# Transposing two chunks of normalised rows by SBUF-to-SBUF transfers, with another list of VectorE's score groups

## The chip, the cores and the metric

The kernel runs on one core of a Trainium2 chip. The metric is the device time of one execution in microseconds, the median of three runs. A core has five engines that run side by side and meet only at semaphores: TensorE (PE, matmul), VectorE (DVE), ScalarE (ACT, exponentials and the like), GpSimd (POOL) and SyncE (SP), which here only issues transfers. Each engine works off its own list of instructions in order.

## The reference

A block with layer norm, attention and a gated multilayer perceptron over 2048 rows of 448 numbers in bf16:

```python
xn = _layernorm(x, axis=-1)
s = _A_ref(xn, A_wqkv, A_wo)      # 16 heads of 28, softmax over 2048 keys
g = _silu(_B_ref(xn, B_w1, B_b1, B_w2, B_b2))   # 448 -> 1792 -> gelu -> 448
return x + s * g
```

Inside `_A_ref`: `qkv = x @ wqkv`, scores `q . k` times 28 to the power -0.5, softmax, times `v`, times `wo`. The largest part is the exponentials: 16 x 2048 x 2048 of them.

## The kernel before, in words

**Tiling.** The 2048 rows are four chunks `c` of 512 rows, each of four tiles `t` of 128 rows. The 16 heads are four groups `g` of four heads; a head takes 32 rows of the 128, so that four heads' scores can run on four row strips of TensorE. A block is one group and one chunk of queries; 16 blocks make the attention. Within a block a score tile `m` is 128 keys times 512 queries of one head, in a bank of PSUM; there are 16 x 16 x 4 = 1024 of them (`MTOT`).

**Start.** `p_ln` computes mean and variance of a chunk's rows on VectorE, `p_ln2` normalises the four tiles into `xn` (VectorE the even tiles, GpSimd the odd ones from chunk 1 on; lines L706 and L710). `xn` lies inside the buffer `h` and has three slots, chunk `c` in slot `c % 3`. The matmuls need the features on the partitions, so `xn` is transposed into `xnT`: for chunk 0 in `p_first`, for chunks 1 to 3 in `p_tr`, twice per chunk: eight TensorE transposes against the identity into one PSUM bank (`t_tr`, L724) and one VectorE copy of 128 x 1024 to `xnT` (`t_trev`, L735). Then `p_k`, `p_q` and `p_v0` project keys, queries and values (L744, L1031), with VectorE evicting them (L755, L983, L1041). Later the rest of the projections and the first layer of the perceptron (`p_f1`, matmul L1089, eviction L1072) are worked in between the scores.

**Exponentials.** `p_scores` (L1223) puts two or three score tiles in one of the two halves of the PSUM ring; `p_exps` lets ScalarE exponentiate such a unit in one instruction (L1279) into a slot of `P`, or later of `h` and `xnT`. `p_pv` multiplies with the values into `acc` (L1494).

**VectorE's groups.** `QUADS` lists the groups of four score tiles (`m = 4q` to `4q + 3`) whose exponential VectorE computes instead of ScalarE: `p_late` sends their scores to any free bank, `p_apass` evicts each with a scale and an offset as 16-bit integers (L1382), and `p_expq` finishes the four together with five operations (L1433 to L1440).

**What sets the order.** The order of every engine's instructions is fixed before the launch by a planner (`run`): each piece of work is a Python generator that yields tasks with a planned duration; the planner puts the task that could start first, with priorities, and emits the waits on semaphores that follow from the buffers (`deps`, `mark`). Tasks that wait for a transfer use a planned time of landing. `until` conditions are tested against planned times. An engine then runs its list in that order whatever the real times are. Transfers are issued by SyncE in the order in which they were planned; a wait holds up all that is behind it in that list.

**Transfers.** At the start SyncE issues all loads of `x`, `wqkv`, then `b2`, `w1` (1344 KB and 224 KB), then copies of `x` into the output for the final addition; `wo` follows once GpSimd has cleared it, `w2` late.

**End.** `p_epi` and `p_norm4` normalise a block, `p_out` and `p_last` multiply by `wo`, multiply by the gate and add to the output.

Of the kernel before, what the change touches and what calls it, by code (L numbers as in the profile page):

```python
# [11 lines left out]
PE, ACT, DVE, POOL, SP = ET.PE, ET.Activation, ET.DVE, ET.Pool, ET.SP  # L12
# [7 lines left out]
C = 4  # L20
# [7 lines left out]
MTOT = NBLK * T * 4  # L28

GM = 64 * 9 + 6  # L30
QUADS = (17, 22, 25, 36, 37, 59, 65, 72, 82, 87, 99, 103, 115, 122, 129, 135, 138, 142, 152, 153, 157, 158, 164, 168, 178, 180, 194, 199, 211, 213, 222, 229, 234, 242)
SM_SCALE = DH ** -0.5
LOG2E = 1.4426950408889634
EXP_A3, EXP_A2, EXP_LC = 0.16391228, 0.00783292, 1.1187538523466403
# [12 lines left out]
SEM, OWN = 0.07, 0.03  # L47
SWITCH = 0.1
JOINT = 0.05
LEAD, WAIT, GLEAD = 0, 3.0, 48  # L50
EPS = 0.1

# [24 lines left out]
class _Kernel:  # L77
# [183 lines left out]
    def alloc(self):  # L261
# [117 lines left out]
        self.s_x = [self.sem("s_x%d" % q) for q in range(4)]  # L379
        self.s_x2 = [self.sem("s_x2%d" % q) for q in range(4)]  # L380
        self.s_b1 = self.sem("s_b1")
        self.s_qn = [[self.sem("s_qn%d_%d" % (q, c)) for c in range(C)] for q in range(G)]
        self.s_x0b, self.s_wqk1 = self.sem("s_x0b"), self.sem("s_wqk1")
        self.s_out = [self.sem("s_out%d" % q) for q in range(10)]
# [2 lines left out]
    def schedule(self):  # L387
        K = self
        K.n_f1 = 0
        K.exp_u = -1  # L390
        K.exp_m = -1
        K.late_ready = []
        K.sc_u = -1
        K.pv_m = -1
        K.E_done = -1
        K.norms_done = False
        K.stg_done = 0
        K.qsqs = [0, 1]
        K.qn = [[] for _ in range(G)]
        K.qn_done = 0  # L400
        K.q0_done = 0
        K.f2n = [0] * C
        K.pv_started = False
        K.chunks_done = 0
        K.g_done = [False] * C
        K.on_done = [False] * NBLK
        K.on4 = [False] * 4
        K.ln_done = 0
        K.taken = 0
        K.next_m = 0  # L410
        K.n_late = 0
        K.gu = None
        K.pend = None
        K.units = []
        K.pv_done = [False] * MTOT
        K.late = {4 * q + k for q in QUADS for k in range(4)}
        K.late_left = [sum(1 for q in QUADS if K.sub_of(4 * q) == b) for b in range(NBLK + 3)]
        K.late_on = False
        K.PB, K.PPREV, K.plast = {}, {}, {}
        K.free_u = []  # L420
        K.a_left = {}
        K.ln2e = 0
        K.late_blk = 0
        K.banks += [(K.ring[:, b, :], K.b_ring[b]) for b in (3, 2)]
        K.outs = []
        K.gelu_done = False
        K.dir_n = 0
        K.dir_read = 0
        self.constants()
        self.loads()  # L430
        for c in range(C):
            K.spawn(K.p_ln(c), c)
        K.spawn(K.p_first(), 0)
        K.spawn(K.p_scores(), 0)
        K.spawn(K.p_take(2), 0)
        K.spawn(K.p_exps(), 0)
        K.spawn(K.p_pv(), 0)
        K.spawn(K.p_units(), 0)
        K.spawn(K.p_late(), 0)
        K.spawn(K.p_busy(), 100)  # L440
        o = 1.0

        def nxt():
            nonlocal o
            o += 1.0
            return o
        K.spawn(K.p_norms(), nxt())
        for c in range(1, C):
            K.spawn(K.p_tr(c, 0), nxt())
            K.spawn(K.p_tr(c, 1), nxt())  # L450
            K.spawn(K.p_k(0, c), nxt())
            if c == 1:
                K.spawn(K.p_v0(0), nxt())
            K.spawn(K.p_v0(c), nxt())
        K.spawn(K.p_q(0, 1), nxt())
        for c in (2, 3):
            K.spawn(K.p_q(0, c), nxt())
        for c in range(C):
            K.spawn(K.p_k(1, c), nxt())
        K.spawn(K.p_q(1, 0), nxt())  # L460
        for t in range(T):
            K.spawn(K.p_v1(t), nxt())
        for c in (1, 2, 3):
            K.spawn(K.p_q(1, c), nxt())
        K.spawn(K.p_qn(1), nxt())
        f1 = deque(SBT)
        for c in range(C):
            for _ in range(4):
                K.spawn(K.p_f1(*f1.popleft()), nxt())
            K.spawn(K.p_k(2, c), nxt())  # L470
            K.spawn(K.p_q(2, c), nxt())
        K.spawn(K.p_qn(2), nxt())
        while f1:
            K.spawn(K.p_f1(*f1.popleft()), nxt())
        for c in range(C):
            K.spawn(K.p_k(3, c), nxt())
            K.spawn(K.p_q(3, c), nxt())
        K.spawn(K.p_qn(3), nxt())
        K.spawn(K.p_gelu(), 0)
        K.spawn(K.p_direct(), 0)  # L480
        for c in range(C):
            for t in range(4):
                K.spawn(K.p_f2(c, t), nxt())
            K.spawn(K.p_silu(c), nxt())
        K.o_epi = 0.5
        for c in range(C - 1):
            for t in range(4):
                K.spawn(K.p_out(c, t), nxt())
        for t in range(4):
            K.spawn(K.p_last(t), nxt())  # L490
        K.run()
        for h in K.outs:
            K.wait(SP, h)
# [92 lines left out]
    def loads(self):  # L586
        K = self

        def ld(dst, src, sem, w, land):
            return K.dma(SP, lambda eng: eng.dma_start(dst, src), sem, writes=w, land=land)  # L590
# [16 lines left out]
            ld(K.x_sb[:, c, :, :], xr[c], K.s_x[c], [K.b_x[c]], 8.0 + 1.8 * c)  # L607
        lw(4 * DH, D, K.s_wqk1, K.b_stg1, 16.5)

        ld(K.b2b[:, :], K.B_b2.partition_broadcast(128), K.s_w["b"], [K.b_b2], 20)  # L610
        ld(K.w1[:, 0:3, :], K.B_w1[0:384, :].rearrange("(kt p) f -> p kt f", p=128), K.s_w["w1"], [], 0)
        ld(K.w1[0:64, 3, :], K.B_w1[384:448, :], K.s_w["w1"], [K.b_w1], 30)

        def out_x():
            yield ("until", lambda: K.late_on)
# [67 lines left out]
    def p_ln2(self, c, h, ts):  # L683
        K = self
        sl = slice(4 * c + ts[0], 4 * c + ts[-1] + 1)
        if c < 2:
            yield _Task(ACT, lambda eng: eng.activation(K.lnv[:, sl], K.mv[:, sl, 1], ACTF.Ln, bias=K.epsc[:, 0:1]),
                        [K.b_mv[c][h], K.b_pads], [K.b_ln[c][h]], 0.3, 0.0, 2 if c else 0)
            yield _Task(ACT, lambda eng: eng.activation(K.rstd[:, sl], K.lnv[:, sl], ACTF.Exp, scale=-0.5),
                        [K.b_ln[c][h]], [K.b_rs[c][h]], 0.2, 0.0, 2 if c else 0)  # L690
        else:
            yield _Task(POOL, lambda eng: eng.tensor_scalar(K.lnv[:, sl], K.mv[:, sl, 1], LN_EPS, None, op0=ALU.add),
                        [K.b_mv[c][h]], [K.b_ln[c][h]], 0.24, 0.05, 0)
            yield _Task(POOL, lambda eng: eng.tensor_tensor(K.rstd[:, sl], K.lnv[:, sl],
                                                            K.mhalf[:, 0:1].to_broadcast([128, len(ts)]), ALU.pow),
                        [K.b_ln[c][h], K.b_pads], [K.b_rs[c][h]], 1.1, 0.05, 0)
        if len(ts) == 4:
            K.b_rs[c][1] = K.b_rs[c][0]
        if c > 0:
            yield _Task(POOL, lambda eng: eng.tensor_scalar(K.nm[:, sl], K.mv[:, sl, 0], -1.0, None, op0=ALU.mult),  # L700
                        [K.b_mv[c][h]], [K.b_nm[c][h]], 0.22, 0.05, c)
        for t in ts:
            i = 4 * c + t
            rd = [K.b_x0[h] if c == 0 else K.b_x[c], K.b_mv[c][h], K.b_rs[c][h], K.b_pads]
            if c == 0 or t % 2 == 0:
                yield _Task(DVE, lambda eng, i=i, t=t: eng.tensor_scalar(  # L706
                    K.xn[:, c % 3, t, 0:D], K.x_sb[:, c, t, :], K.mv[:, i, 0:1], K.rstd[:, i:i + 1],
                    op0=ALU.subtract, op1=ALU.mult), rd, [K.b_xn[c % 3][t]], 0.38, 0.05, c)
            else:
                yield _Task(POOL, lambda eng, i=i, t=t: eng.tensor_scalar(  # L710
                    K.xn[:, c % 3, t, 0:D], K.x_sb[:, c, t, :], K.nm[:, i:i + 1], K.rstd[:, i:i + 1],
                    op0=ALU.add, op1=ALU.mult), rd + [K.b_nm[c][h]], [K.b_xn[c % 3][t]], 0.7, 0.05, c)
        K.ln_done += len(ts) // 2

    def t_tr(self, c, pr, h, bank, tok, prio=5):
# [240 lines left out]
    def p_tr(self, c, pr):  # L956
# [5 lines left out]
        K.banks.append((bank, tok))  # L962
        K.chunks_done += 1

    def boot(self):
        return self.b_qT[0][1].tw is not None

# [358 lines left out]
    def may_join(self, r):  # L1326
# [7 lines left out]
        st = K.start_of(p["task"])  # L1334
        return st is not None and max(r["tok"].tr, r["tok"].tw or 0.0) + SEM <= st + JOINT

# [15 lines left out]
    def p_late(self):  # L1352
        K = self
        yield ("until", lambda: K.late_on)
        K.spawn(K.p_room(), 0)
        for q in QUADS:
            m0 = 4 * q
# [325 lines left out]
```

## Time and profile before

The time is 461.31 us, the median of three runs (460.98 to 461.32). The profiled execution spans 459.3 us.

| what | before |
|---|---|
| time | 461.31 us |
| TensorE busy | 436.3 us, 95%, of it 34.3 us of filler matmuls (L905) |
| VectorE busy | 373.1 us, 81% |
| ScalarE busy | 446.8 us, 97% |
| GpSimd busy | 40.9 us, 9% |
| exponentials on ScalarE (L1279) | 362 instructions, 418.8 us busy |
| TensorE transposes of chunks 1 to 3 (L724) | 48, median 219 ns |
| their VectorE copies (L735) | 6 of about 0.69 us |
| VectorE's group evictions (L1382) | 136 of about 0.69 us |

Busy time counts an instruction from its start to its end, and neighbouring instructions of an engine overlap a little. A row of the groups by line names the line of the program, the engine, the operation, what it writes and reads, its shape, how often it ran, and its busy time and mean. In the timeline the first two numbers of a row are the start and the length in microseconds; `x6` after the names means that six instructions in sequence are merged in the row. A row of the windows gives, for a stretch of time, its length and each engine's busy time and number of instructions. A row of the waits names who waited, for whom, the total, how often, and the longest.

### The profile page before, as it was taken

How to read it: one execution, taken by the hardware profiler on the slowest of the kernel's cores; microseconds unless marked ns; L12 is line 12 of the kernel's file. 1: busy time of each engine (PE TensorE's matmuls, PEld its weight loads, DVE VectorE, ACT ScalarE, POOL GpSimd, SP SyncE). 2: the span in 40 equal slices, each digit the busy share in tenths (PEclk: the TensorE clock that was granted, in tenths of full speed). 3: DMA queues.
4: the chain of work that ended last, by engine and by line, in shares of the span. 5: the costliest groups of instructions: out<-in, count | busy, mean ns of one | idle time of the engine just before them, and what ended most of it. 6: DMA issues, size and time to landing. Idle time of an engine off the chain costs nothing.

```text
span 459.3 us, 10615 instructions
## 1 busy us (share of the span) xinstructions
PE 436.3 (95%) x4431; PEld 162.2 (35%) x4431; DVE 373.1 (81%) x584; ACT 446.8 (97%) x408; POOL 40.9 (9%) x85
## 2 busy tenths in 40 slices
PE   6999999999999999999999999999999999989994
PEld 5543333333332323323333333333323334343452
DVE  8956898894897798878989989847778978999965
ACT  5999999999999999999999999999999999999994
POOL 7470000000000000000000000000000100101111
PEclk9999999999999999999999999999999999999998
DMA  8701000000000000000050000000000001300331
GB/s 269 268 2 37 2 0 1 1 1 4 1 1 0 1 2 3 1 2 1 0 143 1 2 0 2 1 1 0 1 1 2 1 0 42 43 1 1 42 43 41
DMA packets 8050, 11.16 MB, mean 24 GB/s; under 512 B 1698, under 2 KB 6994, under 8 KB 7955
## 3 DMA queue, kind: packets, MB, share of 16 engines
q1 hardware_dynamic: 6850, 8.43, 6.1%
q0 software_dynamic: 864, 1.38, 2.4%
q8 instruction: 35, 0.57, 0.5%
q10 hardware_dynamic: 288, 0.69, 0.4%
q14 instruction: 13, 0.10, 0.1%
HBM read 8.61 MB, written 3.21 MB: 26 GB/s over the span
## 4 chain that ended last, share of the span: by engine, by line
PE 47%; ACT 38%; issue 11%; DVE 3%; POOL 1%; ACTq 0%; DVEq 0%; POOLq 0%
ACT P L1279 18%; PE ring L1223 13%; ACT xnT L1279 9%; ACT h L1279 9%; PE acc L1494 8%; PE ring L1089 5%; PE ring L1158 3%; PE misc L1158 3%; PE acc L905 3%; PE misc L1089 2%; PE misc L744 2%; PE ring L744 2%; PE acc L887 1%; PE misc L1223 1%; PE ring L1031 1%
## 5 line engine op out<-in xcount | busy, mean ns | idle before, releaser
L1279 ACT ACTIVATE P<-ring 128x1024 bf16<-128x1024 f32 (+1 forms) x188 | 217.6, 1265 | 1.4 <-PE ring L1223 1.0
L1223 PE MATMUL ring<-qT,kT 32*128 32x512 bf16 (+2 forms) x1074 | 145.1, 358 | 11.4 <-ACT P L1279 5.6
L1279 ACT ACTIVATE h<-ring 128x1024 bf16<-128x1024 f32 (+1 forms) x102 | 117.8, 1268 | 0.2
L1223 PEld LDWEIGHTS ring<-qT,kT 32*128 32x128 bf16 x1074 | 37.6, 91 | 134.2 <-ACT P L1279 55.7
L1279 ACT ACTIVATE xnT<-ring 128x1536 bf16<-128x1536 f32 (+1 forms) x72 | 83.4, 1308 | 0.0
L1494 PE MATMUL acc<-P,vaug 128*32 128x512 bf16 (+2 forms) x524 | 49.2, 358 | 0.0
L1089 PE MATMUL ring<-xnT,w 128*128 128x512 bf16 x156 | 41.4, 382 | 1.1 <-ACT h L1138 0.9
L1564 POOL CAST rhi<-rc 128x16 bf16<-128x16 f32 x15 | 6.0, 400 | 365.2 <-DVE rc L1562 297.0
L905 PE MATMUL acc<-ident,zero 128*128 128x128 bf16 x393 | 34.3, 221 | 0.0
L1223 PE MATMUL misc<-qT,kT 32*128 32x512 bf16 (+1 forms) x78 | 29.1, 376 | 0.0
L905 PEld LDWEIGHTS acc<-ident,zero 128*128 128x128 bf16 x393 | 22.3, 97 | 18.8 <-issue 18.2
L1494 PE MATMUL acc<-h,vaug 128*32 128x512 bf16 x248 | 27.6, 384 | 0.0
L1158 PE MATMUL misc<-w,h 128*128 128x448 bf16 x112 | 27.3, 356 | 0.0
L1158 PE MATMUL ring<-w,h 128*128 128x448 bf16 x112 | 27.2, 355 | 0.0
L1382 DVE TENSOR_SCALAR x_sb<-misc 128x512 uint16<-128x512 f32 x31 | 21.3, 686 | 6.2 <-PE misc L1223 5.9
L1089 PE MATMUL misc<-xnT,w 128*128 128x512 bf16 x68 | 19.5, 383 | 0.5 <-DVE qT L1581 0.5
L1552 DVE CAST E_sb<-acc 128x512 bf16<-128x512 f32 x15 | 10.4, 690 | 11.7 <-PE acc L1494 11.7
L1494 PE MATMUL acc<-xnT,vaug 128*32 128x512 bf16 (+2 forms) x240 | 18.7, 330 | 0.9 <-ACT P L1279 0.7
L1089 PEld LDWEIGHTS ring<-xnT,w 128*128 128x128 bf16 x156 | 12.1, 97 | 20.0 <-issue 7.2
L1494 PEld LDWEIGHTS acc<-P,vaug 128*32 128x32 bf16 x524 | 11.8, 94 | 15.0 <-issue 11.8
L1382 DVE TENSOR_SCALAR kT<-ring 128x512 uint16<-128x512 f32 x19 | 13.1, 688 | 4.3 <-PE ring L1223 3.4
L1138 ACT ACTIVATE h<-h 128x2048 bf16<-128x2048 bf16 (+2 forms) x8 | 16.2, 2029 | 0.0
(269 smaller groups left out, 663.2 us busy)
## 6 DMA issues: line engine op xcount, KB each, us to landing
w<-in_B_w_dram SPq DMA_DIRECT2D x1, 1568.0 KB, 7.6
w<-in_B_w_dram SPq DMA_DIRECT2D x1, 1344.0 KB, 8.6
out_dram<-in_A_x_dram SPq DMA_DIRECT2D x3, 448.0 KB, 10.7
out_dram<-h POOLq DMA_DIRECT2D x6, 224.0 KB, 3.9
x_sb<-in_A_x_dram SPq DMA_DIRECT2D x2, 448.0 KB, 5.0
h<-in_A_wqkv_dram SPq DMA_DIRECT2D x3, 168.0 KB, 5.1
x_sb<-in_A_x_dram ACTq DMA_DIRECT2D x1, 448.0 KB, 4.4
h<-in_A_x_dram SPq DMA_DIRECT2D x1, 448.0 KB, 4.3
```

What stands on the lines that cost most here:

```text
L744: ins = eng.matmul(bank, w[:, kt, g * 128:(g + 1) * 128], K.xnT[:, kt, c * 512:(c + 1) * 512], start=(kt == 0), stop=(kt == KT - 1))
L887: yield _Task(PE, lambda eng: eng.matmul(bank[:, 0:256], K.ident[:, :], K.E_sb[:, 0, 0:256], start=True, stop=True), [K.b_id, K.b_pads], [ ...
L905: ins = eng.matmul(K.acc[:, 0:128], K.zero[:, :], K.ident[:, :], start=False, stop=True, skip_group_check=True)
L1089: ins = eng.matmul(bank, K.w1[:, kt, ft * 128:(ft + 1) * 128], K.xnT[:, kt, c * 512:(c + 1) * 512], start=(kt == 0), stop=(kt == KT - 1))
L1138: yield _Task(ACT, lambda eng, dst=dst, src=src: eng.activation(dst, src, ACTF.Gelu_apprx_tanh), rd, wr, 0.4267 * n + (0.1 if pc else 0.06 ...
L1158: ins = eng.matmul(ps, hv[:, ft, t * 128:(t + 1) * 128], K.w2[:, ft, :], start=(ft == 0), stop=(ft == FT - 1))
L1223: return eng.matmul(dst, K.kT[32 * j:32 * j + 32, g, t * 128:(t + 1) * 128], K.qT[32 * j:32 * j + 32, g, c * 512 + q0:c * 512 + q0 + nq], ...
L1279: return eng.activation(reg[:, i0:i0 + n, :], K.ring[:, b0:b0 + n, :], ACTF.Exp, scale=SM_SCALE)
L1382: yield _Task(DVE, lambda eng: eng.tensor_scalar(K.unit[u][:, 512 * k:512 * k + 512].bitcast(dt.uint16), bank, SM_SCALE * LOG2E * 128.0, ( ...
L1494: return eng.matmul(K.acc[32 * j:32 * j + 32, q0:q0 + nq], K.vaug[:, t, 4 * g + j, :], ap[:, col:col + nq], tile_position=(0, 32 * j), sta ...
L1552: yield _Task(DVE, lambda eng: eng.tensor_copy(E, K.acc[:, :]), [K.b_acc], [tE], 0.7, 0.0, 0)
L1564: yield _Task(POOL, lambda eng: eng.tensor_copy(K.rhi[:, :], K.rc[:, :]), [K.b_rc], [K.b_rhl], 1.1, 0.0, 1)
```

## The change

For chunks 2 and 3 the sixteen transposes and two copies of a chunk are replaced by transposing transfers from SBUF to SBUF: one per tile of 128 rows (`p_dtr`), issued by SyncE as soon as the tile is normalised. All four of a chunk count up one semaphore, and the chunk's `xnT` counts as written when the last of them has landed, planned 3.0 us after its tile (`DTL`). This takes the work from TensorE and VectorE. Chunks 0 and 1 stay as they were. So that the transfers don't stand behind the large loads, `b2` and `w1` are loaded after all transposes are issued. The bookkeeping in `xn_c` says which chunk a slot of `xn` holds. The list of VectorE's groups has 33 entries in place of 34; 13 of them are in both lists.

```diff
-QUADS = (17, 22, 25, 36, 37, 59, 65, 72, 82, 87, 99, 103, 115, 122, 129, 135, 138, 142, 152, 153, 157, 158, 164, 168, 178, 180, 194, 199, 211, 213, 222, 229, 234, 242)
+QUADS = (17, 20, 25, 36, 38, 57, 72, 82, 90, 98, 104, 114, 121, 134, 135, 140, 141, 148, 153, 155, 158, 164, 167, 178, 187, 194, 196, 209, 215, 218, 229, 234, 241)
...
+DT, DTL = (2, 3), 3.0
...
         for c in range(1, C):
-            K.spawn(K.p_tr(c, 0), nxt())
-            K.spawn(K.p_tr(c, 1), nxt())
+            if c in DT:
+                K.spawn(K.p_dtr(c), nxt())
+            else:
+                K.spawn(K.p_tr(c, 0), nxt())
+                K.spawn(K.p_tr(c, 1), nxt())
             K.spawn(K.p_k(0, c), nxt())
...
-        ld(K.b2b[:, :], K.B_b2.partition_broadcast(128), K.s_w["b"], [K.b_b2], 20)
-        ld(K.w1[:, 0:3, :], K.B_w1[0:384, :].rearrange("(kt p) f -> p kt f", p=128), K.s_w["w1"], [], 0)
-        ld(K.w1[0:64, 3, :], K.B_w1[384:448, :], K.s_w["w1"], [K.b_w1], 30)
+        def load_w1():
+            yield ("until", lambda: K.chunks_done == 2 * (C - 1))
+            ld(K.b2b[:, :], K.B_b2.partition_broadcast(128), K.s_w["b"], [K.b_b2], K.now + 8)
+            ld(K.w1[:, 0:3, :], K.B_w1[0:384, :].rearrange("(kt p) f -> p kt f", p=128), K.s_w["w1"], [], 0)
+            ld(K.w1[0:64, 3, :], K.B_w1[384:448, :], K.s_w["w1"], [K.b_w1], K.now + 10)
+        K.spawn(load_w1(), 40)
...
+    def p_dtr(self, c):
+        K = self
+        left = [0, 1, 2, 3]
+        while left:
+            yield ("until", lambda: any(K.b_xn[c % 3][t].tw is not None and (c < 3 or K.xn_c[c % 3][t] == c) for t in left))
+            t = min((t for t in left if K.b_xn[c % 3][t].tw is not None and (c < 3 or K.xn_c[c % 3][t] == c)), key=lambda t: K.b_xn[c % 3][t].tw)
+            left.remove(t)
+            last = not left
+            src = K.xn[:, c % 3, t, :].rearrange("n (k p) -> n k p", p=128)
+            dst = K.xnT[:, :, c * 512 + t * 128:c * 512 + (t + 1) * 128]
+            tok = K.b_xn[c % 3]
+            K.deps(SP, [tok[t]], [])
+            K.dma(SP, lambda eng, dst=dst, src=src: eng.dma_start_transpose(dst, src), K.s_tr[c],
+                  reads=tok if last else [], writes=K.b_xnT[c] if last else [], land=max(K.now, tok[t].tw) + DTL)
+            K.chunks_done += 1 if t % 2 else 0
```

More of the change, by code (lines that the diff above doesn't have):

```diff
@@ L381, in alloc @@
         self.s_b1 = self.sem("s_b1")
+        self.s_tr = [self.sem("s_tr%d" % q) for q in range(C)]
         self.s_qn = [[self.sem("s_qn%d_%d" % (q, c)) for c in range(C)] for q in range(G)]
@@ L397, in schedule @@
         K.stg_done = 0
+        K.xn_c = [[-1] * 4 for _ in range(3)]
         K.qsqs = [0, 1]
@@ L703, in p_ln2 @@
             i = 4 * c + t
+            K.xn_c[c % 3][t] = -1
             rd = [K.b_x0[h] if c == 0 else K.b_x[c], K.b_mv[c][h], K.b_rs[c][h], K.b_pads]
@@ L708, in p_ln2 @@
                     op0=ALU.subtract, op1=ALU.mult), rd, [K.b_xn[c % 3][t]], 0.38, 0.05, c)
+                K.xn_c[c % 3][t] = c
             else:
@@ L712, in p_ln2 @@
                     op0=ALU.add, op1=ALU.mult), rd + [K.b_nm[c][h]], [K.b_xn[c % 3][t]], 0.7, 0.05, c)
+                K.xn_c[c % 3][t] = c
         K.ln_done += len(ts) // 2
```

## The prediction

> **What bounds the kernel now.** I read the page's busy shares first, then the windows by stage, then ScalarE's own waits, then the timeline around the place of the change.
>
> ```profile
> PE 436.3 (95%) x4431; PEld 162.2 (35%) x4431; DVE 373.1 (81%) x584; ACT 446.8 (97%) x408; POOL 40.9 (9%) x85
> ```
>
> Two engines are nearly full. TensorE's share holds 34 us of filler matmuls on `acc` (L905, x393), so real matmul work is some 402 us. ScalarE has no filler. By stage:
>
> ```profile
> core 0: us, PE busy (x) PEld busy (x) DVE busy (x) ACT busy (x) POOL busy (x), PEclk, DMA share, GB/s
> 20.00:32.00 12.00, 11.93 (x126) 5.45 (x124) 8.41 (x19) 11.70 (x13) 7.71 (x10) 1.00 0.03 9
> 32.00:45.48 13.48, 13.33 (x109) 4.54 (x111) 7.69 (x15) 13.48 (x15) 3.49 (x4) 1.00 0.15 31
> 276.70:452.80 176.10, 170.44 (x1961) 65.66 (x1959) 140.38 (x198) 175.90 (x156) 11.58 (x20) 1.00 0.08 13
> ```
>
> In these rows ScalarE's column almost equals the width; this holds from the first exponential (12.94 us) to the last (452.18 us), the first 8 us apart. In the stretch that the transposes lie in (20 to 32 us) VectorE is busy only 8.41 of 12 us. ScalarE's own waits behind scores are short:
>
> ```profile
> ACT P L674 <- DMA x_sb<-in_A_x_dram: 2.2, 1, 2.2
> ACT P L1279 <- PE ring L1223: 1.0, 3, 0.5
> ```
>
> The busy column hides small gaps, because one ACTIVATE's tail overlaps the next one's start. The distance between starts is the real price:
>
> ```profile
> 90.49 1.07 ACT L1279 ACTIVATE P<-ring 128x1024 bf16<-128x1024 f32 x1
> 91.39 6.96 ACT L1279 ACTIVATE h<-ring 128x1536 bf16<-128x1536 f32 x6
> 98.24 1.46 ACT L1279 ACTIVATE P<-ring 128x1536 bf16<-128x1536 f32 x1
> 99.57 1.05 ACT L1279 ACTIVATE h<-ring 128x1024 bf16<-128x1024 f32 x1
> ```
>
> A unit of two score tiles takes 0.90 us (90.49 to 91.39), one of three 1.33 us (98.24 to 99.57). The groups by shape give 196 units of two, 165 of three and one of one: 196 x 0.90 + 165 x 1.33 + 0.5 = 396 us for 888 tiles. The time from 12.94 to 452.66 us, less the stretch of GELU and its tables (247.92 to 275.80), the four tanh (6.6) and one layer-norm pair (0.4), is 405 us. So about **8 us of small gaps** are spread over the exponentials. The end is ScalarE's work plus these gaps plus a fixed tail of 6.6 us.
>
> **What the Trainium skill says.** "VectorE: DVE Perf Modes", section "The three transpose paths", lists 390 ns for a 128x128 bf16 transpose on TensorE and 1309 ns for one through the DMA crossbar. The trace has 219 ns for the TensorE one in its pipelined run; no run of before has the other. "DMA: Bandwidth & Descriptors", section "Latency and other measured facts", gives transposing transfers 261 GB/s in one kernel and 350 to 400 when contiguous; nothing in the trace shows it. The same page's "DMA Transpose (X-bar)" demands that only one stream transposes at a time: all eight transfers go out on SyncE, so no wait is added for that. Its section "Why a DMA increments its semaphore by 16 and not by 1" says that of DMAs in flight on one semaphore only the full count proves that all have landed; the change waits for the full count of a chunk's four transfers. The trace can't confirm it.
>
> **The change, part by part.**
>
> *Removed from TensorE and VectorE.*
>
> ```profile
> L724 PE MATMUL misc<-ident,h x24: 218/219/230, 15.2 to 29.5; 128*128 128x128 bf16 x24
> L735 DVE COPY xnT<-misc x3: 673/680/691, 16.7 to 29.8; 128x1024 bf16<-128x1024 bf16 x3
> L735 DVE COPY xnT<-ring x3: 678/692/692, 17.3 to 30.6; 128x1024 bf16<-128x1024 bf16 x3
> ```
>
> Of the 48 transposes, 32 are chunks 2 and 3: eight runs of four at about 0.40 us, 3.2 us of TensorE. Of six copies four go: 4 x 0.69 = 2.7 us of VectorE. Both lie beside ScalarE's exponentials, which run from 21.13 us on without a recorded idle. What is gained on the path is at most the small gaps there: 26 units of two from 21.13 to 45.48 us take 24.35 us against 26 x 0.90 = 23.4 us. Of these 0.9 us I take 0.2 us as gained, since most of the gaps there lie away from the transposes.
>
> *Eight transposing transfers.* Each moves 128 x 512 x 2 B = 131 KB, that is four 128x128 blocks. Low bound: the nearest row, the 112 KB stores of `h`, 1.7 us from issue to landing. High bound: four blocks at the page's 1309 ns one after the other, 5.2 us, with the next transfer behind it. The new code plans 3.0 us after the last tile. Who waits: the K projection of chunk 2, and everything behind it in TensorE's order, scores included.
>
> ```profile
> 20.10 1.03 DVE L706 TENSOR_SCALAR h<-x_sb,mv,rstd 128x448 bf16<-128x448 bf16 x2
> 20.19 1.51 POOL L710 TENSOR_SCALAR h<-x_sb,nm,rstd 128x448 bf16<-128x448 bf16 x2 [0.20 <-POOL nm L700]
> 21.13 14.92 ACT L1279 ACTIVATE P<-ring 128x1024 bf16<-128x1024 f32 x16 [0.30 <-PE ring L1223]
> 23.66 0.68 DVE L735 COPY xnT<-misc 128x1024 bf16<-128x1024 bf16 x1
> 26.09 0.69 DVE L755 CAST kT<-ring 128x512 bf16<-128x512 f32 x1 [0.80 <-PE ring L744]
> 27.87 0.12 PEld L1223 LDWEIGHTS ring<-qT,kT 32*128 32x128 bf16 x2 [0.21 <-issue]
> ```
>
> Chunk 2's last normalised tile is ready at 20.19 + 1.51 = 21.7 us; before, its transpose is complete at 24.34 and its K at 26.78 us. The first score on chunk 2's keys is the 17th unit (four heads times eight key tiles, two to a unit). Counting 1 + 7 units before 21.13 us and 0.92 us for each after it, the 17th exponential starts near 28.5, its score near 27.9 us. The slack is 27.9 - 26.8 = 1.1 us, so the transfers may land until about 24.3 + 1.1 = 25.4 us free of charge. SyncE's issues take about 0.53 us each (two `x_sb` loads in 1.06 us). Four between 20.6 and 22.3 us with 1.7 to 3.2 us to land (the row of a 224 KB load) gives 24.0 to 25.5 us: hidden, just. The high bound gives 20.6 + 4 x 5.2 = 41.4 us: 16 us late. I take 0. Chunk 3 has 1.7 us of slack by the same count (K at 33.57, its first score at 35.3 us).
>
> *The later load of w1, b2 and its place.* It moves from 8.61 us behind the transfers, to near 30 us, and takes 9 us. The first GELU projection is evicted at 102.4 us (L1072), so this costs nothing, nor do the loads of `wo` behind it, which the output projection needs only after 430 us.
>
> *One of VectorE's groups less, the others moved.* The list has 34 entries before and 33 after. A group is four score tiles that VectorE exponentiates (four L1382 of 0.69 us and five operations of 0.69, 0.69, 1.22, 0.69 and 1.22 us, 7.3 us). All four now go to ScalarE. At (0.90 + 1.33) / 5 = 0.446 us per tile that is **+1.78 us** on the engine that sets the end, hidden behind nothing. VectorE had 19% idle before, so the 7.3 + 2.7 us it is freed of buy nothing by themselves. In return the interference of one group goes: the gaps divided by the groups are 8 / 34 = 0.2 us.
>
> *Sum.* +1.8 for the group, -0.2 for its gaps, -0.2 in the start, 0 for the transfers: +1.4 us, 461.3 + 1.4 = **462.7 us**.
>
> **The rivals.**
>
> *A better fit of the groups (faster).* Only 13 of the 33 positions are also in the list before, and the 8 us of gaps depend on where the groups stand. If the gaps fall to 5 us, the result is -3.0 + 1.8 = -1.2 us: 460.1 us. For it: the gaps are bigger than the price of a group, and an early TensorE with 3 us less work lets projections run earlier. Against it: the gaps are scattered and mostly 0.1 to 0.2 us, nothing in the trace ties them to the transposes, and most groups sit in blocks far from them.
>
> *The gaps pay for just the group (no change).* Gaps down by 1.8 us: 461.3 us.
>
> *Late transfers (slower).* The wait on the transpose takes the place of the one on VectorE's copy. If they land 3 us after the slack ends, ScalarE, with at most two units ahead, runs dry and the loss is never made good: 462.7 + 3 = 465.7 us. At the high bound 475 us and more. For it: a slack of only 1.1 us and a price with a ratio of three between its bounds. Against it: transfers share 16 engines, so four in a row need not take four times one.
>
> **How the numbers follow.** Forecast 0.42, better fit 0.28, even 0.12, late transfers 0.18. The forecast's own spread, 461.9 to 463.6 us, gives 0.04 to "no change"; a small part of the better fit adds to faster as its size is open. Faster 0.28, same 0.16, slower 0.56. The range leaves out the deepest part of the better fit and the upper half of the late transfers: 459.5 to 465.8 us.
>
> **What would show it.** Right: ScalarE's exponentials are 892 tiles instead of 888; its start-to-start distances stay 0.90 and 1.33 us; no idle of ScalarE over 0.5 us between 24 and 37 us; the K projections of chunks 2 and 3 don't wait for a DMA; the tail after the last exponential stays near 6.6 us. Late transfers would show as a wait of TensorE's weight loads for `xnT` behind a DMA and as idle of ScalarE near 27 to 36 us. A better fit would show as fewer than 8 us of gaps after 45 us. The forecast is wrong if gaps shift by more than 1 us either way, or if the transfers take over 4 us from the last issue.

## The result, and the profile after

The changed kernel takes **468.73 us** (468.52 to 469.04), the kernel before 461.24 us in the same session: 1.0164 times as long (95% interval in brackets: [1.0146, 1.0182]), or 7.5 us slower. The forecast was 462.7 us, the range ended at 465.8 us: the direction was right, the size was not. Some executions of several kernels here ran at a lower granted TensorE clock and took longer; the ratios, and the ranges given in place of a median, leave these out.

The busy shares of the changed kernel, to be held against 436.3, 373.1 and 446.8 us before:

```profile
PE 437.0 (94%) x4484; PEld 167.2 (36%) x4511; DVE 365.4 (78%) x571; ACT 449.0 (96%) x409; POOL 39.6 (8%) x85
```

VectorE has 7.7 us less to do. TensorE is busy 0.7 us longer, but that includes filler matmuls, which went from 34.3 us (393) to 41.4 us (513); its real work is less. ScalarE has 2.2 us more to do, so most of the 7.5 us must be idle time. By stage (length, then busy time and count of PE, PEld, DVE, ACT, POOL, clock, DMA share, GB/s):

```profile
20.00:32.00 12.00, 9.69 (x105) 4.42 (x103) 5.50 (x14) 10.14 (x12) 9.27 (x12) 1.00 0.51 88
32.00:45.00 13.00, 11.63 (x93) 4.01 (x93) 6.32 (x12) 12.15 (x14) 1.79 (x2) 1.00 0.77 270
```

ScalarE, with 11.70 us busy in the first of these stretches before, is down to 10.14 us; TensorE falls from 11.93 to 9.69 us. ScalarE's waits for TensorE have grown. Those for scores were 1.0 us in total before, 0.5 us the longest; the one for the weighted sum is new (waiter, releaser: total, times, longest):

```profile
ACT P L1307 <- PE ring L1251: 3.5, 5, 1.6
...
ACT h L1307 <- PE acc L1522: 2.0, 1, 2.0
```

L1307 is the exponential (L1279 before), L1251 the score (L1223), L1522 the weighted sum with the values (L1494). The first wait lies at the place of the change, which the timeline shows:

```profile
20.17 10.49 SPq L989 DMA_TRANSPOSE xnT<-h  x8
...
20.78 5.71 ACT L1307 ACTIVATE P<-ring 128x1024 bf16<-128x1024 f32 x6 [0.29 <-PE ring L1251]
...
26.66 0.55 PEld L756 LDWEIGHTS ring<-xnT,wk 128*128 128x128 bf16 x4 [1.83 <-DMA xnT<-h]
28.06 5.61 ACT L1307 ACTIVATE P<-ring 128x1024 bf16<-128x1024 f32 x6 [1.57 <-PE ring L1251]
...
33.11 0.55 PEld L756 LDWEIGHTS ring<-xnT,wk 128*128 128x128 bf16 x4 [1.13 <-DMA xnT<-h]
34.51 1.94 ACT L1307 ACTIVATE P<-ring 128x1024 bf16<-128x1024 f32 x2 [0.85 <-PE ring L1251]
```

SyncE needs 10.49 us for eight issues. The key projections of chunks 2 and 3 (L756) stand in TensorE's list and wait for the transfers, 1.83 and 1.13 us; scores behind them come late, and ScalarE idles 1.57 and 0.85 us.

**A ledger of ScalarE** puts numbers on it. Every exponential starts some distance after the one before; 0.48, 0.904 and 1.33 us are the undisturbed distances for one, two and three tiles. The floor is the number of units times these; gaps are what the distances hold beyond it, split at VectorE's evictions of a block's `acc` into `E_sb`. The parts add up to the span, to within rounding.

| us | before | changed | difference |
|---|---|---|---|
| first exponential starts | 12.94 | 12.59 | -0.35 |
| floor (1, 196, 165 units; 0, 197, 166) | 397.1 | 398.9 | +1.8 |
| gaps in the first block (to 46.2; to 48.8 us) | 0.95 | 3.64 | +2.7 |
| gaps in the second block (to 79.7; to 85.5 us) | 1.06 | 2.87 | +1.8 |
| gaps in all other blocks | 6.3 | 7.4 | +1.1 |
| GELU, tanh, layer norm | 34.3 | 34.3 | 0.0 |
| after the last exponential | 6.64 | 6.88 | +0.2 |
| span | 459.3 | 466.5 | +7.2 |

The earlier first exponential can't be credited to the change: in two of the kernels below that keep the loads of before it lies at 12.59 and at 13.22 us.

The experiments ask what stands behind the gaps: the transfers themselves, their lateness, VectorE, or the order.

### The profile page after: what moved, and what is told of

It reads as the page before. It is cut to its first block, busy times and chain, and to the rows that moved or that the text cites. A ratio compares the mean times of both kernels' runs of the same rounds, so it can differ in the third digit from the quotient of the medians.

```text
span 466.5 us, 10747 instructions
## 1 busy us (share of the span) xinstructions
PE 437.0 (94%) x4484; PEld 167.2 (36%) x4511; DVE 365.4 (78%) x571; ACT 449.0 (96%) x409; POOL 39.6 (8%) x85
## 4 chain that ended last, share of the span: by engine, by line
PE 52%; ACT 30%; issue 9%; DVE 2%; POOL 1%; DMA 1%; ACTq 0%; POOLq 0%; DVEq 0%
PE ring L1251 15%; ACT P L1307 12%; PE acc L1522 9%; ACT h L1307 9%; PE ring L1117 7%; ACT xnT L1307 6%; PE misc L1186 5%; PE acc L917 3%; PE ring L1186 3%; PE misc L1117 2%; PE ring L756 2%; PE misc L756 1%; ACT h L1166 1%; PE misc L1619 1%; PE ring L1619 1%
## 5 line engine op out<-in xcount | busy, mean ns | idle before, releaser
L1307 ACT ACTIVATE P<-ring 128x1024 bf16<-128x1024 f32 (+1 forms) x184 | 212.9, 1271 | 4.1 <-PE ring L1251 3.5
L1251 PE MATMUL ring<-qT,kT 32*128 32x512 bf16 (+2 forms) x1082 | 145.7, 358 | 11.5 <-ACT P L1307 5.2
L1307 ACT ACTIVATE h<-ring 128x1024 bf16<-128x1024 f32 (+1 forms) x107 | 120.4, 1257 | 2.5 <-PE acc L1522 2.0
L1251 PEld LDWEIGHTS ring<-qT,kT 32*128 32x128 bf16 x1082 | 37.6, 91 | 132.6 <-ACT P L1307 52.8
L1307 ACT ACTIVATE xnT<-ring 128x1536 bf16<-128x1536 f32 (+1 forms) x72 | 83.5, 1271 | 0.1
L1522 PE MATMUL acc<-P,vaug 128*32 128x512 bf16 (+2 forms) x519 | 42.0, 357 | 0.0
L917 PE MATMUL acc<-ident,zero 128*128 128x128 bf16 x513 | 41.4, 220 | 0.0
L917 PEld LDWEIGHTS acc<-ident,zero 128*128 128x128 bf16 x513 | 29.2, 98 | 18.1 <-issue 17.0
L1186 PE MATMUL misc<-w,h 128*128 128x448 bf16 x126 | 30.7, 355 | 0.0
L1251 PE MATMUL misc<-qT,kT 32*128 32x512 bf16 (+1 forms) x70 | 26.1, 376 | 0.0
L1522 PE MATMUL acc<-h,vaug 128*32 128x512 bf16 x257 | 25.9, 384 | 0.1
L1410 DVE TENSOR_SCALAR x_sb<-ring 128x512 uint16<-128x512 f32 x31 | 21.2, 685 | 4.3 <-PE ring L1251 4.1
L1186 PE MATMUL ring<-w,h 128*128 128x448 bf16 x98 | 23.0, 355 | 0.1
L1522 PE MATMUL acc<-xnT,vaug 128*32 128x512 bf16 (+2 forms) x240 | 17.4, 330 | 0.7 <-ACT xnT L1307 0.7
L1100 DVE CAST h<-ring 128x512 bf16<-128x512 f32 x18 | 12.3, 686 | 4.6 <-PE ring L1117 4.5
L1522 PEld LDWEIGHTS acc<-P,vaug 128*32 128x32 bf16 x519 | 10.6, 95 | 12.6 <-issue 9.8
```

The lines of the kernel that those rows point to most:

```text
L917: ins = eng.matmul(K.acc[:, 0:128], K.zero[:, :], K.ident[:, :], start=False, stop=True, skip_group_check=True)
L1100: yield _Task(DVE, lambda eng: eng.tensor_copy(dst, bank), [tok], wr, 0.69, 0.0, 2)
L1186: ins = eng.matmul(ps, hv[:, ft, t * 128:(t + 1) * 128], K.w2[:, ft, :], start=(ft == 0), stop=(ft == FT - 1))
L1251: return eng.matmul(dst, K.kT[32 * j:32 * j + 32, g, t * 128:(t + 1) * 128], K.qT[32 * j:32 * j + 32, g, c * 512 + q0:c * 512 + q0 + nq], ...
L1307: return eng.activation(reg[:, i0:i0 + n, :], K.ring[:, b0:b0 + n, :], ACTF.Exp, scale=SM_SCALE)
L1410: yield _Task(DVE, lambda eng: eng.tensor_scalar(K.unit[u][:, 512 * k:512 * k + 512].bitcast(dt.uint16), bank, SM_SCALE * LOG2E * 128.0, ( ...
```

## The experiments

Each ratio is against the kernel before, run on the same chip in the same session. Edits are to the changed kernel unless said, and `...` marks lines left out.

**The old list in the changed kernel, and the new list in the old one.** The first has `QUADS` of before, the second is the kernel before with `QUADS` of after; nothing else.

> The whole change but with the list of 34 groups of the kernel before. Theory A (the transfers are late and cost only their two early gaps; the new list costs the rest): ScalarE's two gaps near 25 and 33 us stay at 1.7 and 1.0 us, 888 tiles on ScalarE, some 461.3 + 2.7 - 0.35 = 463.6 us. Theory B (the late transfers upset the order of everything behind them, so that the gaps after 45 us come from them too): 468.7 less one group of 1.8, some 466.9 us. Theory C (the list alone costs it all): 461.3 us.

> The kernel before with only the list of 33 groups, nothing else of the change. Theory A: one group more on ScalarE (+1.8 us) and the gaps that the new positions bring, above all the one of 2.3 us near 82 us: 465 to 466 us. Theory B: only the group, 463.1 us, with small gaps like those of before. Theory C: 468.7 us.

Measured 478.29 us, 1.0371 [1.0357, 1.0385], and 470.39 us, 1.0199 [1.0186, 1.0213]. The first misses every expectation; the second is nearest to its theory C, 1.7 us beyond. By the ratios, the new list alone costs 9.2 us in the old kernel, and the transfers with the old list cost 17.1 us, 9.6 us more than with the new one. So the two parts of the change don't add up (9.2 and 17.1 us apart, 7.5 together): a list and the order that the planner makes of it belong together. ScalarE's waits of the first of these kernels show what kind of loss it is:

```profile
ACT h L1307 <- PE acc L1522: 5.6, 2, 5.2
ACT P L1307 <- PE ring L1251: 4.3, 8, 2.1
ACT P L1307 <- PE acc L1522: 3.3, 1, 3.3
```

**Planned landing of 6 us in place of 3.**

```diff
-DT, DTL = (2, 3), 3.0
+DT, DTL = (2, 3), 6.0
```

> The changed kernel, with a landing planned 6.0 us after the tile in place of 3.0 us, which is near what the trace of after shows (5.2 and 6.0 us after the last tile). The transfers are the same. Theory A1 (the loss near 25 and 33 us comes from the projection standing in TensorE's list ahead of scores that don't need the transfer): TensorE's waits for the transfers fall from 3.0 us to under 0.5 us, the two gaps from 2.7 us to under 1 us together, 466.5 to 467.5 us if nothing later changes. Theory A2 (the keys are needed at that time anyway): the gaps stay at some 2.7 us, 468.7 us.

Measured 469.71 us, 1.0188 [1.0174, 1.0202]. TensorE no longer waits for any transfer, but the time is no better: the planner puts the projection of chunk 2 later (it starts at 29.39 us, 2.4 us after chunk 2 has landed), and the keys are then missing. The timeline of this kernel has the two gaps of the first block as one:

```profile
31.69 2.85 ACT L1307 ACTIVATE P<-ring 128x1024 bf16<-128x1024 f32 x3 [2.98 <-PE ring L1251]
```

Planning for lateness moves the loss; it doesn't remove it.

**The kernel before with the late load of w1 and b2** (the `load_w1` of the change).

> The kernel before with only the later load of w1 and b2; transposes on TensorE, the old list. Theory A: the exponentials begin 0.35 us earlier, as in after, because the early loads of x have less beside them: 460.9 us. Rival: the earlier start of after is chance or comes from elsewhere: 461.3 us. If the load in the middle of the start disturbs a transfer that is waited for: over 461.8 us.

Measured 461.0 us, 0.9998 [0.999, 1.0006]: no difference.

**Only chunk 3 by transfers.**

```diff
-DT, DTL = (2, 3), 3.0
+DT, DTL = (3,), 3.0
```

> The changed kernel with only chunk 3 transposed by transfers, chunk 2 by TensorE as before; list of 33. Theory A (each issue holds SyncE for 1.27 us, and chunk 2's four in a row are what makes it late): the gaps in the first block fall from 3.6 us to 1.0 to 2.0 us, chunk 3's last transfer lands 5 to 6 us after its tile. Rival (a transfer's own 2.5 us to landing is what is late, whatever stands before it): the chunk 3 gap stays at 1.0 us and the first block at some 2 us. What the second block does depends on the order that the planner rebuilds: 1 to 6 us there.

Measured 476.5 us, 1.0339 [1.0323, 1.0356]. The planner makes another order: 8.05 us of gaps in the first block, more than with two chunks. The expectation failed, and the run can't tell transfers from order. What follows is only that from here on an experiment must keep the order.

**Sixteen half transfers.** Each tile of 128 x 512 goes in two transfers of 128 x 256; the compute engines' lists are unchanged.

```diff
-            src = K.xn[:, c % 3, t, :].rearrange("n (k p) -> n k p", p=128)
+            for k in range(2):
...
+                src = K.xn[:, c % 3, t, 256 * k:256 * (k + 1)].rearrange("n (k p) -> n k p", p=128)
...
```

> The changed kernel with each transposing transfer cut in two (two 128x128 blocks each instead of four, sixteen in place of eight); the order on all computing engines is the same. If SyncE's 1.27 us per issue grow with the number of blocks: 0.65 us each, the last landing and the time unchanged, 468.7 us. If they are mostly a fixed price: near 1.2 us each, chunk 2 lands some 5 us later than 26.6 us, and the time grows by some 7 to 10 us as chunk 3 is pushed back as well.

Measured 488.05 us, 1.0596 [1.058, 1.0613]. The rows of the issues (ns min, median, max; first and last start in us), that of the changed kernel first:

```profile
L989 SPq DMA_TRANSPOSE xnT<-h x8: 1189/1266/1310, 20.2 to 29.4; - x8
...
DMA to landing us min/median/max: 2.4/2.5/3.7
```

```profile
L991 SPq DMA_TRANSPOSE xnT<-h x16: 1231/1246/1937, 20.3 to 40.3; - x16
...
DMA to landing us min/median/max: 2.3/2.4/4.0
```

Half the bytes take the same issue time, so twice as many transfers take twice as long on SyncE. This run shows the price of an issue, about 1.25 us for two blocks and 1.27 us for four, as the thing that spaces the transfers. Of the 19.0 us that the span grows, 18.5 are gaps in the first block (22.1 against 3.6); the other blocks are as in the changed kernel.

**One of VectorE's groups less.**

```diff
-QUADS = (17, 20, 25, 36, 38, ...
+QUADS = (17, 25, 36, 38, ...
```

> The changed kernel with 32 groups, the one at 20 (in the second block) left to ScalarE. Theory A (in the second block ScalarE runs out of buffers because the multiplication with the values waits for VectorE's three groups): the gaps of the second block fall from 2.9 to about 1 us, the floor grows by 1.8 us: 468.6 us, no loss from having one group less. Rival (VectorE's groups aren't what that stage waits for): the gaps stay, 470.5 us.

Measured 485.33 us, 1.0539 [1.0515, 1.0564]. Both expectations fail, by 15 us and more: the order is upset as in the runs above.

**The transfers beside the old work.** The kernel before with the eight transposing transfers added into a region that is not yet in use; the order on the compute engines is that of before, and nobody waits for them in the start.

> The kernel before, in its own order on every computing engine, with the eight transposing transfers added beside it into memory that is free at that time; nobody waits for them in the start. Theory A (issuing and moving cost nothing, only the wait for them does): 461.2 us, no change. Rival (the transfers slow the engines' own memory accesses or the loads): over 461.7 us. Their issues should take the same 1.27 us and land by 27 and 33 us.

Measured 461.29 us, 1.0007 [0.9999, 1.0015]. The transfers themselves, with their traffic in SBUF, cost nothing that is clear of the noise here.

**The removed work, taken out in place.** The kernel before, order kept; half of the 32 transposes, and 15/16 of each of the four copies are gone. The matmuls that used this data read columns of chunks 0 and 1 instead.

```diff
-                for t in (2 * h, 2 * h + 1):
+                for t in (2 * h, 2 * h + 1)[:1 if c > 1 else 2]:
...
-        return _Task(E, lambda eng: eng.tensor_copy(dst, psb), [tok], [K.b_xnT[c][pr]], 0.7, 0.0, prio)
+        return _Task(E, lambda eng: eng.tensor_copy(dst if c < 2 else dst[:, :, 0:32], psb if c < 2 else psb[:, :, 0:32]), [tok], [K.b_xnT[c][pr]], 0.7, 0.0, prio)
...
```

> The kernel before, same order on every engine, with most of the work that the change removes taken out in place: of the 32 transposes of chunks 2 and 3 on TensorE 16 are left, and VectorE's four copies carry 32 columns of each half instead of 512 (the projections of chunks 2 and 3 read the columns of chunks 0 and 1, so that half of the keys are those of other data). Theory A (the removed work lies beside ScalarE and buys only part of the small gaps there): 460.9 to 461.2, within 0.2 us of before. Theory B (it frees TensorE and VectorE where they set the pace): 460.0 or less, a gain of over 1 us that the changed kernel then lost elsewhere.

Measured 460.93 us against 460.96, 1.0 [0.9991, 1.0008]. Half of what the change takes off TensorE, and nearly all that it takes off VectorE, is worth nothing where it lies; the other half of the transposes was not taken out.

**One transfer per chunk**, 16 blocks each, with `xnT` of chunks 2 and 3 kept tile by tile.

```diff
...
-                  reads=tok if last else [], writes=K.b_xnT[c] if last else [], land=max(K.now, tok[t].tw) + DTL)
+            if last:
+                src = K.xn[:, c % 3, :, :].rearrange("n t (k p) -> n (t k) p", p=128)
+                dst = K.xnT[:, c, :].rearrange("p (b n) -> p b n", n=128)
+                K.deps(SP, tok, [])
+                K.dma(SP, lambda eng: eng.dma_start_transpose(dst, src), K.s_tr[c],
+                      reads=tok, writes=K.b_xnT[c], land=max(K.now, tok[t].tw) + DTL)
...
```

> The changed kernel, list of 33 and the same order on every computing engine, but each chunk's four transposing transfers made one (sixteen 128x128 blocks, issued when the last tile is normalised; the two chunks of xnT are kept tile by tile instead of by feature block, so that one transfer can write them). The run with halved transfers showed a fixed 1.25 us for each issue. Theory A (the lateness is the four issues in a row): the issue takes near 1.3 us, chunk 2 lands by 25 us in place of 26.6, TensorE's waits for the transfers fall from 3.0 us to under 1 us, the first block's gaps fall from 3.6 to 1 to 1.5 us, 466.0 to 466.8 us. Rival (a transfer of sixteen blocks takes its blocks one by one, 0.3 us or more each): no gain, or up to 4 us slower than 468.7 us. What the second block loses (2.9 us) and the group (1.8 us) stay in either case.

Measured 469.02 to 470.5 us, 1.0192 [1.0178, 1.0207]; the profiled span is 466.6 us, that of the changed kernel 466.5.

```profile
L1006 SPq DMA_TRANSPOSE xnT<-h x2: 1933/2010/2086, 21.5 to 27.3; - x2
...
DMA to landing us min/median/max: 4.3/5.1/5.8
```

SyncE spends 4 us in place of 10, but sixteen blocks take 4.3 to 5.8 us to land. Chunk 2 comes 0.7 us earlier, chunk 3, issued at 27.3 us when its last tile is normalised, is there at 33.1 us as before, and the time doesn't gain. So this run does not show what a cheaper issue alone is worth.

**The transfers, but early.** The decisive run keeps every instruction of the compute engines in its place and takes the lateness away: the transfers read rows of `x` as loaded, so that they need not wait for the layer norm.

```diff
-            src = K.xn[:, c % 3, t, :].rearrange("n (k p) -> n k p", p=128)
+            src = K.x_sb[:, c, :, :].rearrange("n t d -> n (t d)")[:, 416 * t:416 * t + 512].rearrange("n (k p) -> n k p", p=128)
...
-            K.deps(SP, [tok[t]], [])
+            pass
...
-                  reads=tok if last else [], writes=K.b_xnT[c] if last else [], land=max(K.now, tok[t].tw) + DTL)
+                  reads=[K.b_x[c]], writes=K.b_xnT[c] if last else [], land=max(K.now, tok[t].tw) + DTL)
```

> The changed kernel, but the eight transposing transfers read rows of x as loaded, not the normalised rows, so they need not wait for the layer norm and land several us earlier; the numbers of chunks 2 and 3 are therefore those of other data. Every instruction of the four compute engines stands in the same order as in the changed kernel. Theory A (late transfers cost what ScalarE idled in the first block, 2.7 us more than before): no TensorE wait for xnT behind a DMA, gaps of the first block at about 1.0 us instead of 3.6, time 468.7 - 2.7 = 466.0. Theory B (the order itself holds the gaps, as with the transfers planned at 6 us, or later slack takes the gain back): gaps move elsewhere, 468.2 to 469.0. Theory C (all of the loss above the group is the transfers): 463.1.

Measured **466.11 us**, 1.011 [1.0096, 1.0124]: theory A to 0.1 us. The timeline of this kernel at the same place:

```profile
20.93 13.16 ACT L1307 ACTIVATE P<-ring 128x1024 bf16<-128x1024 f32 x14 [0.29 <-PE ring L1251]
...
25.21 0.55 PEld L756 LDWEIGHTS ring<-xnT,wk 128*128 128x128 bf16 x4 [0.23 <-issue]
...
30.75 0.55 PEld L756 LDWEIGHTS ring<-xnT,wk 128*128 128x128 bf16 x4 [0.23 <-issue]
```

Fourteen exponentials follow each other where the changed kernel has two gaps. TensorE comes to the projections at 25.21 and 30.75 us; in the changed kernel the data are there at 26.66 and 33.11 us. Chunk 3 is thus 33.11 - 30.75 = 2.4 us late against an undisturbed run, chunk 2 only 1.45 us, and the later chunk sets the loss. That is why the earlier chunk 2 of the single transfers bought nothing. Gaps of the first block fall from 3.64 to 1.14 us; all later blocks keep theirs to within 0.02 us. The loads behind the transfers start earlier here too (that of `b2` at 21.55 in place of 30.71 us); the last pair of runs below moves them alone, and the span changes by 0.4 us.

**VectorE's work in the second block.** The changed kernel, order kept, with the five operations of group 25 cut from 2048 to 64 columns.

```diff
-        bT, bD, bW = K.b_U[u], K.b_U[uv[0]], K.b_U[uv[1]]
+        bT, bD, bW = K.b_U[u], K.b_U[uv[0]], K.b_U[uv[1]]; (T, D1, W) = (x[:, 0:64] if m0 == 100 else x for x in (T, D1, W))
```

> The changed kernel with the five operations of VectorE's group 25 cut from 2048 to 64 columns (the rest of that group's probabilities is left out), in the same order on every engine. It takes some 3.5 us of VectorE out of the stretch from 76 to 84 us. Theory A (in the second block VectorE is full and ScalarE waits for the weighted sum behind that group): the gap of 2.3 us at 82 us goes, gaps of the second block about 0.9 instead of 2.9, time 468.7 - 1.8 = 466.9. Theory B (that gap has another cause, or is made good later): 468.5 to 469.

> Both at once: transfers from rows as loaded, and group 25 cut to 64 columns, same order. Theory A (two separate losses, each carried to the end): 468.7 - 2.7 - 1.8 = 464.2, which leaves 1.8 for the group's four tiles on ScalarE and 1.1 for small gaps. Theory B (one hides the other, or later waits take over): 466 to 467.

Measured 469.08 us, 1.0171 [1.0157, 1.0185], and with both edits 465.95 us, 1.0104 [1.0091, 1.0118], against 466.11 us for the early source alone. **My theory fell.** The gap in the second block stays at 2.87 us. The timeline of the run with the narrow group says why:

```profile
82.02 1.61 ACT L1307 ACTIVATE P<-ring 128x1536 bf16<-128x1536 f32 x1
...
82.08 0.19 DVE L1468 TENSOR_TENSOR w<-w,x_sb 128x64 bf16<-128x64 f16 x1
...
83.68 0.39 PE L1251 MATMUL ring<-qT,kT 32*128 32x512 bf16 x3 [0.18 <-ACT P L1307]
...
84.28 0.39 PE L1522 MATMUL acc<-h,vaug 128*32 128x512 bf16 x1
...
85.67 1.02 ACT L1307 ACTIVATE h<-ring 128x1024 bf16<-128x1024 f32 x1 [2.05 <-PE acc L1522]
```

VectorE ends the group at 82.27 us, 2.0 us before the weighted sum (L1522) begins. The sum stands in TensorE's list behind the scores of 83.68 us, these wait for ScalarE's exponential of 82.02 to 83.63 us to free their half of the ring, and ScalarE's next exponential waits for the sum to free its slot in `h`. ScalarE waits for TensorE, TensorE for ScalarE: the gap is in the order of the lists, and less work on VectorE did not remove it.

**The order alone.** The kernel before with one planned duration changed. No operation does more or less; only the number of filler matmuls follows the plan (516 in place of 393).

```diff
-        return _Task(E, lambda eng: eng.tensor_copy(dst, psb), [tok], [K.b_xnT[c][pr]], 0.7, 0.0, prio)
+        return _Task(E, lambda eng: eng.tensor_copy(dst, psb), [tok], [K.b_xnT[c][pr]], 0.6, 0.0, prio)
```

> The kernel before with one number of the planner changed: the copy of the transposes is planned at 0.6 us instead of 0.7; no operation's work changes, only the order that the planner writes. Theory A (the list of groups fits one order alone, and any disturbance of the order costs): some 470, about 9 us slower than before, as much as the planner itself plans. Theory B (only real work and real waits count): 461.2.

Measured 468.59 us, 1.0162 [1.0147, 1.0178]. A tenth of a microsecond in a plan costs as much as the whole change. The waits of ScalarE in the first 100 us of this kernel have the same releaser as the second block above:

```profile
ACT P L1279 <- PE acc L1494: 1.6, 1, 1.6
ACT h L1279 <- PE acc L1494: 1.2, 1, 1.2
```

**The early load of w1 again**, in the changed kernel and in the one with a transfer per chunk (the lines of `load_w1` go back to the three of before).

> The changed kernel with the loads of b2 and w1 back in their early place, ahead of the transposing transfers instead of right behind them; same order on every compute engine. Theory A (the loads issued behind the transfers share the DMA engines with chunk 3's last transfers, which is why those take 3.7 us to land and chunk 2's only 2.4): chunk 3 lands about 1.2 us earlier, its wait of 1.0 us on ScalarE goes, time about 467.6. Theory B (chunk 3's transfers are slow for another reason): 468.7, landings unchanged.

> One transposing transfer per chunk as tried before, and the loads of b2 and w1 early as in the run beside this one; same order on every compute engine. Theory A (the loads were what slowed chunk 3's single transfer from 4.3 to 5.8 us): both chunks land 0.7 to 1.5 us earlier than in the changed kernel, gaps of the first block about 1.5 us, time 466.6 to 467. Theory B: 468.7.

Measured 468.57 us, 1.0178 [1.0156, 1.0199], and 468.27 to 468.75 us, 1.016 [1.0142, 1.0177]. The slowest landing falls from 3.7 to 3.4 us and the span by 0.4 us in the first; in the second the landing takes 6.0 us after 5.8. The loads behind the transfers are at most a small part of their slowness.

The traces point to something else. In the changed kernel the first seven transfers land in 2.4 to 2.5 us; only the eighth, the last of chunk 3, takes 3.7 us. While it is under way, one packet of 16 KB runs from 30.37 to 31.55 us on a queue that the profile names `instruction`, and packets of the transfer take up to 1.18 us, against 0.05 us in the seven before. With sixteen half transfers it is the twelfth, from 34.46 to 38.46 us, that takes 4.0 us, and the DMA rows of this stretch hold such a packet and nothing else beside the transposing transfers (queue, kind: packets, MB, share of 16 engines):

```profile
q1 hardware_dynamic: 849, 0.19, 24.4%
q8 instruction: 1, 0.02, 1.6%
```

In all kernels here whose transfers read the normalised rows, those of two or four blocks that met such a packet (of 16 KB, once of 8 KB) before their last tenths took 2.9 to 4.4 us, and all others 2.3 to 2.5 us. So neither the loads nor the copies of `x` behind the transfers are needed for a slow landing. No run moved the packet, so this is a coincidence seen each time, not a tested cause.

## Why the prediction was wrong

**The group, +1.8 us: right.** The units hold 197 x 2 + 166 x 3 = 892 tiles, the distances stayed, and the floor rose by 1.8 us.

**The removed work, -0.2 us in the start: right in kind.** Half of the transposes and nearly all of the copying are worth 0.0 us with the order kept. The late load of w1 at 0 is right as well.

**The transfers, 0 us: wrong; 2.6 us.** The step that failed is "SyncE's issues take about 0.53 us each (two `x_sb` loads in 1.06 us)". A transposing transfer took 1.27 us to issue. The rest of the working for chunk 2 held: the limit of 25.4 us was good (TensorE comes at 25.21 us), and the landing of 2.5 us lies inside the assumed 1.7 to 3.2 us. But the fourth issue starts at 24.13 us, 4.0 us after the first and not 1.6, and lands at 26.62 us. With issues of 0.53 us it could have gone out when its tile was ready, at 21.4 us, and by this estimate would have landed near 23.9 us, in time.

For chunk 3 I gave "1.7 us of slack" from the old order and never worked out when it would land. Its issues don't stand behind those of chunk 2: the last of these ends at 25.40 us, and chunk 3's first tile is normalised at 25.51 us. But its own four at 1.27 us put the last one at 29.39 us, 2.3 us after its tile (27.11 us). With a landing of 2.5 us it would be there at 31.9 us, 1.1 us late against 30.75. TensorE, held up by chunk 2, gets there at 33.11 - 1.13 = 32.0 us, so this lateness alone would have been covered. What it then waits for is the rest of a landing of 3.7 us, outside the assumed range. So, as an estimate, about 1.5 of the 2.6 us are the price of the issue by itself; the other 1.1 us come from the slow landing of one transfer on top of it. Both bounds for the landing were given, none for the issue, and that was the term that mattered.

The range had the mechanism: the rival of late transfers gave +3 us where the early source shows 2.6. Its 3 us were set, not worked out from an issue or a landing, so that the size came so near is luck.

**The other gaps, -0.2 us: wrong; +2.9 us.** The step that failed is "the interference of one group goes: the gaps divided by the groups". Gaps are no property of a group. With the transfers early, 466.11 - 461.05 = 5.1 us are still lost, 1.8 of them the group; the rest is 1.8 us in the second block, 1.1 us in all others, and some tenths at the ends. The narrow group shows that the one in the second block is no work of VectorE, and the planned 0.6 us show that a change of order alone can cost 7.5 us. The rival of a better fit looked at the same term, but only on its lucky side; that lists fitted to another order must be expected to lose was not considered.

The sum is then 1.8 + 2.6 + 2.9 + 0.2 = 7.5 us. The sum is of rounded terms; the last 0.2 holds the tail, the earlier start and what the profile leaves out of the time.

**What stays open.** Whether a list exists that serves the order with transfers as well as the old list serves the old one, so that only the 1.8 and 2.6 us would remain, is not shown; of the versions run none beats the kernel before. Whether the packet on the `instruction` queue is what holds up the last transfer was not tested. How the 1.1 us of gaps in the other blocks come about was not followed up.

## What to carry to other kernels

A transfer that replaces compute work has three prices: the issue on its queue, the landing, and the place where its first reader stands in an in-order list. Multiply the issue by the number of transfers ahead of the last one, from the time that their data are ready, and compare with the time at which the reader's engine gets there, for each chunk and for the last one above all. Where a static order goes with a list of exceptions, as here, expect any edit to the planning to draw a new order, here 1.6 to 5.4% slower than the kernel before each time, and test parts of it only with the order held fixed.

## What the runs showed of the hardware

Issuing a transposing SBUF-to-SBUF transfer occupied SyncE for 1.25 us with two 128 x 128 blocks, 1.27 us with four and about 2.0 us with sixteen, against 0.53 us for a plain load of 448 KB. Landing took 2.3 to 2.5 us for two or four blocks and 4.3 us for sixteen when nothing came between, far less than four times as long, so the blocks of one transfer overlap. Landings of 2.9 to 4.4 us for two or four blocks went with a packet on the `instruction` queue in the same stretch. "VectorE: DVE Perf Modes", section "The three transpose paths", of the Trainium skill gives 1309 ns for one 128x128 block; no run here has a single block, but four cost 1.27 us of the queue and 2.5 us to land, so four times the page's figure, the high bound of the prediction, is not what four blocks take, and the measurement decides.
